# Clustered attention and two MLPs: sums over keys by matrix products, and a new order of the work around a head's value products

## The chip, the cores and the metric

The kernel runs on one core of one Trainium2 chip. The metric is the device time of one launch in microseconds (us). Engines are named as in the profile: PE (TensorE), DVE (VectorE), ACT (ScalarE), POOL (GpSimd), SP (SyncE, which issues DMAs).

## What is computed

Attention over 2 batches x 8 heads, 768 tokens, 64 features, in which a query sees only the keys of its own cluster; then two MLPs over the 1536 tokens. Cut to what matters:

```python
q_assign = argmax(q_n . c_n)            # 16 centroids per head, all normalised
k_assign = argmax(k_n . c_n)
mask = q_assign[:, :, :, None] == k_assign[:, :, None, :]
scores = where(mask, (q . k) / sqrt(D), -1e9)
scores = scores - max(scores, axis=-1)
attn = exp(scores)
attn = attn / (sum(attn, axis=-1) + 1e-9)
x = reshape(attn . v)                   # 1536 x 512
x = (silu(x @ w_in)) @ w_out            # d_ff 2048
out = (sigmoid(x @ w_gate) * (x @ w_val)) @ w_out2   # d_ff 1536
```

## The kernel before

**Tiles.** Heads come in 8 pairs p with j = 0, 1; head h = 2p + j, so there are 16. Tokens are cut into NT = 6 tiles of 128. Every fp32 operand of a product is split into a high part and the rest, so a score is the sum of a product of high tiles `qb`, `kb` (112 rows: 96 of features, 16 of the cluster mask) and one of low tiles `qa`, `ka` (97 rows; the last of `qa` holds the negated maximum of each query). Scores are computed with keys on the partitions, so the sum over keys, the softmax denominator, runs over partitions.

**One head on PE**, in an order written out by hand (`tc.manual_schedule`):

- `leading_maximum(h, i)`, i = 0 to 5 (L456, L466): two products of 384 columns into an `s` tile (two buffers), whose maximum DVE takes into `nm`.
- `shift_row(h, late, w)` (L476): transposes of those maxima into `r`, one for query tiles 0 and 1 (early) and one for tiles 2 to 5 (late); ACT puts them as a row into `qa`.
- `unit(h, u)`, u = 0 to 8 (L490, L497): scores `t`, then exp on ACT into `ring` (`ph` in the rows, two heads deep). Units 0 to 2 need the early row, units 3 to 8 the late one. All `t`, `r`, `pm`, `ps`, `pt` and `n` tiles share three PSUM buffers.
- `values(h)` (L539): 12 fp32 products of 384 columns with `ring`, 24 pieces in the trace.

The value products of head h-1 stand inside head h, after its unit 2 and its last two maxima. They are followed by `denominator_rows(h-2)` (L524), by the late row of head h and by units 3 to 8, among which the first four maxima of head h+1 stand.

**Denominators.** `denominators(h)` (L510 to L513): for each half of the queries DVE adds three key tiles to three (1152 elements a partition), and POOL adds the three results in two steps into `sum`. Six small products with `one_of` (L524) add over the partitions, and ACT casts them to `dn`. `finish(p)` sends both heads' denominators through DRAM, so that DVE can invert them on 96 partitions (`rs`, L569, L570), reads them back broadcast into `rb`, and POOL multiplies (`acc`, L579). The last two heads do without DRAM: `inverse` (L622) adds over the partitions with a tile of ones, and DVE inverts (`rd`).

**The next pair** is prepared meanwhile: cluster products and their turn (`clusters` L153, `turned` L164), `choice` and `one_hot` on DVE (L416 to L429, result `oh`), `mask_rows` (PE L439, ACT L441, four DMAs), `split` (five POOL operations, L404, L68, L407, L408) and DMAs that copy the parts into the tiles (`leading`, `following`, on SP's queue).

The other engines' order is made by a scheduler from the program's order and its own estimates of time; `tc.issue_after(x)` keeps an instruction behind x. Around the last head, weights for the MLPs are loaded and split as well (`ci`, `co`, `wi0a`, `wi0b`, `wo`: ACT, DVE, POOL).

Of the kernel before, what the change touches and what calls it, by code (L numbers as in the profile page):

```python
# [31 lines left out]
def clustered_attention_then_two_mlps(ctx, tc, qT, kT, v, cen, cenT, w1i, w1o, w2g, w2v, w2o, out):  # L32
# [5 lines left out]
    P = 128  # L38
# [72 lines left out]
    with ExitStack() as att:  # L111
# [124 lines left out]
        with tc.issue_after(diagonal.ins):  # L236
            constants(0)
            constants(1)
            one_of = cp.tile([P, GT, D], F32, tag="one_of", name="one_of")
            nc.gpsimd.memset(one_of, 0.0)  # L240
            all_ones = cp.tile([P, D], F32, tag="all_ones", name="all_ones")
            nc.gpsimd.memset(all_ones, 1.0)
            for c in range(GT):
                nc.gpsimd.memset(one_of[:, c, c : c + 1], 1.0)
# [60 lines left out]
        nc.scalar.activation(qh, qq, AF.Copy, scale=scale)  # L305
        cast(nc.scalar, kh, kk)
        nc.vector.tensor_tensor(kl, kk, kh, op=ALU.subtract)
        nc.vector.scalar_tensor_tensor(ql, qq, scale, qh, op0=ALU.mult, op1=ALU.subtract)
# [19 lines left out]

        def first_choice(j, seen):
            sg = seen.rearrange("p (w j c) -> p j w c", j=2, c=C)[:, j]  # L330
            wq, mw = yield from ranked(0, j, sg, 2 * NT)
            for n in range(2):
                nc.vector.tensor_tensor(
                    oh[0][:, :, j, n, 0:C],
                    wq.rearrange("p (t n) c -> p n t c", n=2)[:, n],
                    mw.rearrange("p (t n) -> p n t", n=2)[:, n].unsqueeze(2).to_broadcast([P, NT, C]),
                    op=(ALU.not_equal, ALU.is_equal)[n],
                )
# [17 lines left out]
        def first_masks():  # L356
            with tc.issue_after(maxima[NT - 1].ins):
                for _ in first_choice(1, sums):
                    pass
# [3 lines left out]
            query_rows(1, pt, 0, 0, NT // 2)  # L363
            key_rows(nc.vector, 1, pt, 0, 0, NT)
            query_rows(1, pt, NT // 2, NT // 2, NT // 2)
# [5 lines left out]
        nc.scalar.activation(ex, unit_norm[:, 0:1], AF.Exp)  # L371
        half = NT // 2
# [63 lines left out]
        def mask_rows(p):  # L436
# [5 lines left out]
            for j in range(2):  # L442
                for n, t in enumerate(high[p % 2]):
                    a = 64 * n + 32 * j
                    dma(t[masks, j].bitcast(F32), rows[a : a + C])
# [36 lines left out]
        def unit(h, u):  # L482
# [14 lines left out]
            x = nc.scalar.activation(ring[:, kts[0] : kts[-1] + 1, h % 2, c], t, AF.Exp)  # L497
# [4 lines left out]
        sums_of = {}  # L502

        def denominators(h):

            s = wk.tile([P, S], F32, tag="sum", name=f"sum{h}")
            for g in range(2):
                c = slice(g * G, (g + 1) * G)
                d = wk.tile([P, 3, G], F32, tag="d", name=f"d{h}_{g}", bufs=1)
                nc.vector.tensor_tensor(d, ring[:, 0:3, h % 2, c], ring[:, 3:6, h % 2, c], op=ALU.add)  # L510
                eng = nc.vector if h == NH - 1 else nc.gpsimd
                eng.tensor_tensor(s[:, c], d[:, 0], d[:, 1], op=ALU.add)  # L512
                summed.append(eng.tensor_tensor(s[:, c], s[:, c], d[:, 2], op=ALU.add))  # L513
            sums_of[h] = s

        xf, dn = {}, {}

        def denominator_rows(h, o):

            s = sums_of.pop(h)  # L520
            for c in range(GT):
                for g, r in enumerate((L, U)):
                    at = g * G + c * P
                    nc.tensor.matmul(  # L524
                        o[r], lhsT=one_of[:, c, :], rhs=s[:, at : at + P], start=c == 0, stop=c == GT - 1
                    )
            p, j = divmod(h, 2)
            if p not in dn:
                dn[p] = fin.tile([P, 2, P], F32, tag="dn", name=f"dn{p}", bufs=1)
            r = slice(0, D + GT)  # L530
            cast(nc.scalar, dn[p][r, j], o[r])
# [26 lines left out]
        def finish(p):  # L558

            b, hp = divmod(p, HP)  # L560
            d = dr.tile([2, GT, 2, P], F32, tag="d", name=f"d{p}")
            e = dr.tile([2, GT, 2, P], F32, tag="e", name=f"e{p}")
            n = dn.pop(p)
            dma(d[0], n[0:GT])
            dma(d[1], n[D : D + GT])
            rows = 2 * GT * 16
            rs = fin.tile([P, 16], F32, tag="rs", name=f"rs{p}")
            dma(rs[0:rows], d.rearrange("g c j (a s) -> (g c j a) s", s=16)[0:rows])
            nc.vector.tensor_scalar_add(rs[0:rows], rs[0:rows], 1e-9)  # L569
# [47 lines left out]
        def inverse(h, sums):  # L617

            o = ps_t.tile([P, 512], F32, tag="t", name=f"n{h}")
            for n, s in enumerate(sums):  # L620
                for g, r in enumerate((L, U)):
                    nc.tensor.matmul(  # L622
                        o[r, 0:G],
                        lhsT=all_ones,
                        rhs=s[:, g * G : (g + 1) * G],
                        start=n == 0,
                        stop=n == len(sums) - 1,
                    )
# [24 lines left out]

        shift_row(0, False, P)
        leading_maximum(0, 2)
        clusters(1)
        unit(0, 0)
        leading_maximum(0, 3)
        unit(0, 1)
        leading_maximum(0, 4)  # L660
        unit(0, 2)
        leading_maximum(0, 5)
        turned(1)
        split(1)
# [3 lines left out]
        shift_row(0, True, P)  # L668
        first_masks()
# [4 lines left out]
        def rest_of(h):  # L674

            k = h + 1
            more = k < NH
            for u, i in ((3, 0), (4, 1), (5, None), (6, 2), (7, None), (8, 3)):
                unit(h, u)
                if i is not None and more:  # L680
                    leading_maximum(k, i)
                if u == 6:
                    if h % 2 == 0 and (h + 2) // 2 < NPAIR:
                        mask_rows((h + 2) // 2)
                    if more:
                        shift_row(k, False, P)
                working()

        def prepare(p):
            if p < NPAIR:  # L690
                clusters(p)
# [4 lines left out]
        leading_maximum(1, 0)  # L696
        leading_maximum(1, 1)
        unscaled(0, values(0))
        shift_row(1, False, D)
        choice(1, maxima[NT + 1])  # L700
        one_hot(1, maxima[NT + 1])
        unit(1, 0)
        leading_maximum(1, 2)
        unit(1, 1)
        leading_maximum(1, 3)
        mask_rows(1)
        unit(1, 2)
        leading_maximum(1, 4)
        leading_maximum(1, 5)
        denominators(0)  # L710
        shift_row(1, True, P)
        rest_of(1)
        prepare(2)

        for h in range(2, NH):
            p = (h + 3) // 2
            unit(h, 0)
            denominators(h - 1)
            if h == 2:
                turned(2)  # L720
                for j in range(2):
                    leading(2, j)
                    following(2, j)
            elif p < NPAIR:
                if h % 2:
                    turned(p)
                    leading(p, 0)
                    following(p, 0)
            if h % 2 == 0 and 2 < (h + 2) // 2 < NPAIR:
                leading((h + 2) // 2, 1)  # L730
                following((h + 2) // 2, 1)
            unit(h, 1)
            leading_maximum(h, 4)
            unit(h, 2)
            leading_maximum(h, 5)
            if h == 2:
                choice(2, maxima[-1])
                one_hot(2, maxima[-1])
            elif h % 2 and p < NPAIR:
                choice(p, maxima[-1])  # L740
            elif h % 2 == 0 and (h + 2) // 2 < NPAIR:
                one_hot((h + 2) // 2, maxima[-1])
            o = values(h - 1)
            if h < NH - 1:
                denominator_rows(h - 2, o[:, G:])
                unscaled(h - 1, o)
            else:
                denominator_rows(h - 2, ps_t.tile([P, 512], F32, tag="t", name=f"n{h - 2}")[:, 0:P])
                xo = fin.tile([P, S], F32, tag="xf", name=f"xo{h - 1}")
                cast(nc.scalar, xo[:, 0:G], o[:, 0:G])  # L750
            if h % 2 and h > 1:
                finish((h - 3) // 2)
                if (h - 3) // 2 == HP - 1:
# [537 lines left out]
```

## Time and profile before

| | us |
|---|---|
| three runs | 850.74, 844.76, 850.70 |
| median | 850.7 |
| the profiled execution | 846.96 |
| its span (first to last instruction) | 845.2 |

The span falls into three parts by the starts of the value products: up to those of head 1 (57.8 us), thirteen heads up to those of head 14 (263.3), the way from there into the first MLP (to 318.7, the first product of its second step), and the MLPs. The profile names a tile as written and as read (out<-in), the line of the code, and, for idle time, the instruction that ended it. PEclk is the clock granted to TensorE, 1.00 for 2.4 GHz and 0.50 for 1.2 GHz.

### The profile page before, as it was taken

Reading aid. Unit: us, or ns where it says so; the run is one execution under the profiler, and the core shown is the slowest. Engines: PE = TensorE matmul, PEld = TensorE weight load, DVE = VectorE, ACT = ScalarE, POOL = GpSimd, SP = SyncE. Lnnn points to the kernel's source line nnn. Section 1 sums busy time; section 2 is a strip of 40 time slices with the busy share of each in tenths; the row PEclk is TensorE's granted clock in tenths of the full one; section 3 lists DMA queues with packets and bytes.
Section 4 is the critical chain, followed back from the end, with each engine's and each line's share of the span. In section 5 each row is a group of like instructions: output and inputs, shape, how many; then the busy total and the mean of one; then the engine's idle time right before and its main releaser. Section 6 shows DMA issues by size and latency. Waiting matters only on the chain.

```text
span 845.2 us, 11109 instructions
## 1 busy us (share of the span) xinstructions
PE 774.5 (92%) x4179; PEld 653.5 (77%) x4179; DVE 640.3 (76%) x714; ACT 371.7 (44%) x610; POOL 465.8 (55%) x402
## 2 busy tenths in 40 slices
PE   7788988988797369999999999999999999999997
PEld 3455655655565249989989989999899998989896
DVE  5777777766756697387989778799759697988846
ACT  4435535536354426535435424554643333434220
POOL 3446646649668853434756443544557483948320
PEclk9889999989899579999999999999999999999999
DMA  8745564553511220121322222121111221212004
GB/s 216 184 104 160 131 153 111 141 133 85 144 30 51 69 74 26 51 71 55 115 86 76 74 75 75 50 76 67 58 50 50 75 76 51 100 50 74 1 1 150
DMA packets 32202, 72.26 MB, mean 86 GB/s; under 512 B 6570, under 2 KB 12372, under 8 KB 32148
## 3 DMA queue, kind: packets, MB, share of 16 engines
q1 hardware_dynamic: 31604, 71.52, 28.6%
q8 instruction: 33, 0.54, 0.3%
q14 instruction: 21, 0.17, 0.1%
q10 hardware_dynamic: 544, 0.03, 0.0%
HBM read 48.05 MB, written 3.23 MB: 61 GB/s over the span
## 4 chain that ended last, share of the span: by engine, by line
PE 74%; POOL 7%; DMA 5%; DVE 5%; issue 4%; ACT 2%; SPq 2%; POOLq 0%; DVEq 0%; ACTq 0%
PE z L1107 12%; PE t L490 5%; PE y L1048 4%; PE h_0x L932 3%; PE h_0w L932 3%; PE v L539 3%; PE g_0w L932 2%; PE g_0x L932 2%; PE v_0w L932 2%; PE v_0x L932 2%; PE s L456 2%; PE r L998 2%; PE q L998 2%; PE y_00None L1048 2%; PE y_20None L1048 2%
## 5 line engine op out<-in xcount | busy, mean ns | idle before, releaser
L466 DVE TENSOR_REDUCE nm<-s 128x1 f32<-128x768 f32 x96 | 88.6, 948 | 48.6 <-PE s L456 48.2
L497 ACT ACTIVATE ph<-t 128x512 f32<-128x512 f32 x144 | 82.8, 597 | 35.9 <-PE t L490 35.0
L1107 PE MATMUL z<-wu,ghb 128*128 128x512 f32 (+1 forms) x292 | 89.5, 388 | 0.0
L490 PE MATMUL t<-qa,ka 97*128 97x256 f32 (+1 forms) x192 | 71.6, 383 | 17.3 <-ACT qa L66 13.1
L490 PE MATMUL t<-qb,kb 112*128 112x256 f32 (+1 forms) x192 | 75.0, 401 | 2.3 <-ACT rows L441 2.3
L510 DVE TENSOR_TENSOR d<-ph 128x1152 f32<-128x1152 f32 x30 | 53.6, 1785 | 22.7 <-POOL sum L513 22.7
L539 PE MATMUL v<-ph,vv 128*64 128x384 f32 x384 | 68.9, 500 | 0.0
L512 POOL TENSOR_TENSOR sum<-d 128x384 f32<-128x384 f32 x30 | 30.7, 1024 | 59.6 <-DVE d L510 42.3
L1107 PEld LDWEIGHTS z<-wu,ghb 128*128 128x128 f32 x292 | 54.2, 188 | 11.6 <-ACT ghb L66 0.5
L456 PE MATMUL s<-kb,qb 112*128 112x384 f32 x192 | 53.3, 360 | 8.2 <-DVE nm L466 7.5
L490 PEld LDWEIGHTS t<-qa,ka 97*128 97x128 f32 x192 | 41.4, 216 | 24.4 <-ACT qa L66 22.6
L1107 PE MATMUL z<-wu,glb 128*128 128x512 f32 (+1 forms) x146 | 56.9, 390 | 0.0
L539 PEld LDWEIGHTS v<-ph,vv 128*64 128x64 f32 x384 | 27.3, 139 | 34.2 <-issue 33.7
L490 PEld LDWEIGHTS t<-qb,kb 112*128 112x128 f32 x192 | 41.5, 216 | 12.0 <-ACT rows L441 4.8
L456 PEld LDWEIGHTS s<-kb,qb 112*128 112x128 f32 x192 | 35.6, 204 | 15.3 <-DVE nm L466 10.0
L1028 DVE TENSOR_TENSOR acc<-z,acc 128x1024 f32<-128x1024 f32 (+2 forms) x32 | 36.7, 1153 | 13.9 <-PE z L1107 13.2
L827 POOL TENSOR_TENSOR wo<-co,wo 128x512 fp32r<-128x512 f32 x16 | 23.1, 1449 | 27.0 <-ACT wo L66 27.0
L513 POOL TENSOR_TENSOR sum<-sum,d 128x384 f32<-128x384 f32 x30 | 32.6, 1088 | 0.9
L1048 PE MATMUL y<-gha,wo 128*128 128x384 f32 x128 | 32.8, 334 | 0.0
L1107 PEld LDWEIGHTS z<-wu,glb 128*128 128x128 f32 x146 | 27.4, 188 | 6.9 <-DVE glb L988 1.4
L66 ACT ACTIVATE dn<-v 67x128 f32<-67x128 f32 x13 | 3.6, 273 | 57.4 <-PE v L524 53.7
L808 ACT ACTIVATE co<-ro 128x512 f32<-128x512 f32 x16 | 10.7, 672 | 36.1 <-DMA ro<-in_w1o 33.0
(633 smaller groups left out, 2183.7 us busy)
## 6 DMA issues: line engine op xcount, KB each, us to landing
ri<-in_w1i SPq DMA_DIRECT2D x16, 512.0 KB
ro<-in_w1o SPq DMA_DIRECT2D x16, 512.0 KB, 3.3
rg<-in_w2g SPq DMA_DIRECT2D x12, 512.0 KB, 3.1
rv<-in_w2v SPq DMA_DIRECT2D x12, 512.0 KB, 3.1
ru<-in_w2o SPq DMA_DIRECT2D x12, 512.0 KB, 3.1
qq<-in_qT SPq DMA_DIRECT2D x8, 384.0 KB, 4.8
kk<-in_kT SPq DMA_DIRECT2D x8, 384.0 KB, 4.1
qb<-qh SPq DMA_DIRECT2D x16, 192.0 KB, 2.5
```

Of the source, the lines that this page charges most:

```text
L456: nc.tensor.matmul(s[:, g, 0:HS], lhsT=q[0 : LAST + C, j, i * P : (i + 1) * P], rhs=k[0 : LAST + C, j, g * HS : (g + 1) * HS], start=True, ...
L466: maxima.append(nc.vector.tensor_reduce(n, s[:, :, 0:HS], axis=AX.XY, op=ALU.max, negate=True))
L490: nc.tensor.matmul(t[:, n], lhsT=k[0:rows, j, kt * P : (kt + 1) * P], rhs=q[0:rows, j, c], start=m == 0, stop=m == 1,)
L497: x = nc.scalar.activation(ring[:, kts[0] : kts[-1] + 1, h % 2, c], t, AF.Exp)
L510: nc.vector.tensor_tensor(d, ring[:, 0:3, h % 2, c], ring[:, 3:6, h % 2, c], op=ALU.add)
L513: summed.append(eng.tensor_tensor(s[:, c], s[:, c], d[:, 2], op=ALU.add))
L539: m = nc.tensor.matmul(o[r, 0:G], lhsT=heads[p][:, j, kt, :], rhs=ring[:, kt, h % 2, g * G : (g + 1) * G], start=kt == 0, stop=kt == NT - 1,)
L932: nc.tensor.matmul(o[:, b, 0:HS], lhsT=w[a][s][:, k, :], rhs=right[b, q][t][:, k, :], start=start and k == 0 and n == 0, stop=k == KQ - 1 ...
L998: nc.tensor.matmul(o[:, h, 0:HS], lhsT=w[f"a{m + 1}{r + 1}"][s][:, k, :], rhs=right[b, f"{r + 1}{h + 1}"][t][:, k, :], start=r == 0 and k ...
L1028: added.append(nc.vector.tensor_tensor(z, o, z, op=ALU.add))
L1048: nc.tensor.matmul(o[:, d, 0:width], lhsT=s[:, d, k, :], rhs=t[:, c], start=k == 0 and m == 0, stop=k == 1 and m == 2,)
L1107: nc.tensor.matmul(o[:, a, c], lhsT=s[:, q * P : (q + 1) * P], rhs=r[:, c], start=k == 0 and m == 0, stop=k == 1 and m == 2, skip_group_ch ...
```

## The change

- **Denominators.** DVE adds key tile n+3 to n in three sums of 768 elements into `d` (L513 of the changed kernel). POOL adds nothing any more. PE takes all three in six products of 384 columns with a tile of ones (L522), in a PSUM tile of their own, `n`, from the three shared buffers. They now belong to the head whose values were just taken.
- **Rows of maxima.** All six maxima of head h+1 are computed inside head h's work (`ahead`). The late row of head h is transposed before the value products of head h-1, and the early row of head h+1 right behind them.
- **`split`.** The two high parts are cast on ACT; POOL does the two subtractions alone. The softmax scale moves from `split` into exp.
- **`choice`** for the next pair runs at an even head, `one_hot` and `mask_rows` at the odd head behind it, each one head sooner. `finish` is cut in two: `collect` (to DRAM and back into `rs`) at the even head, the inversion and the rest at the odd one, which held all of it before.
- **The last two heads** have no DVE or POOL sums: `inverse` takes the six key tiles of `ring` directly, twelve products each. That of head 14 stands right behind its values, that of head 15 ahead of its values.
- At the start, maxima come before the first row, and the second head's choice is split in two.

Cut to its core:

```diff
-        def split(p):
+        def split(p, behind=None):
             qq, kk = raws.pop(p)
             qh, ql, kh, kl = parts(p)
-            nc.gpsimd.tensor_scalar(qq, qq, scale, 1.0, op0=ALU.mult, op1=ALU.mult)
-            cast(nc.gpsimd, kh, kk)
-            cast(nc.gpsimd, qh, qq)
-            nc.gpsimd.tensor_tensor(kl, kk, kh, op=ALU.subtract)
-            on_pool["split", p] = nc.gpsimd.tensor_tensor(ql, qq, qh, op=ALU.subtract)
+            cast(nc.scalar, kh, kk)
+            cast(nc.scalar, qh, qq)
...
+                nc.gpsimd.tensor_tensor(kl, kk, kh, op=ALU.subtract)
+                on_pool["split", p] = nc.gpsimd.tensor_tensor(ql, qq, qh, op=ALU.subtract)
...
-        def denominators(h):
...
+        def sums(h):
+
+            d = wk.tile([P, 3, S], F32, tag="d", name=f"d{h}", bufs=1)
+            for n in range(3):
+                summed.append(
+                    nc.vector.tensor_tensor(d[:, n], ring[:, n, h % 2], ring[:, n + 3, h % 2], op=ALU.add)
+                )
+            sums_of[h] = [d[:, n] for n in range(3)]
+
+        def denominators(h, terms):
+
+            o = ps_t.tile([P, 512], F32, tag="t", name=f"n{h}")
+            for n, s in enumerate(terms):
                 for g, r in enumerate((L, U)):
...
+                        o[r, 0:G],
+                        lhsT=all_ones,
+                        rhs=s[:, g * G : (g + 1) * G],
...
+        def inverse(h):
+
+            o = denominators(h, [ring[:, kt, h % 2] for kt in range(NT)])
             rd = fin.tile([P, S], F32, tag="rb", name=f"rd{h}")
...
+        def stretch(h):
+            o = values(h)
+            denominator_rows(h)
+            unscaled(h, o)
...
+        for h in range(2, NH - 1):
...
+            sums(h - 1)
             unit(h, 0)
+            ahead(k, 0)
...
             unit(h, 1)
...
             unit(h, 2)
+            ahead(k, 1)
...
             shift_row(h, True, D)
+            stretch(h - 1)
+            shift_row(k, False, D)
...
+            for u, i in ((3, 2), (4, None), (5, 3), (6, 4), (7, None), (8, 5)):
+                unit(h, u)
+                if i is not None:
+                    ahead(k, i)
...
+        o = values(h - 1)
+        xo = fin.tile([P, S], F32, tag="xf", name=f"xo{h - 1}")
+        cast(nc.scalar, xo[:, 0:G], o[:, 0:G])
+        rd = inverse(h - 1)
         while work:
             working()
         for u in range(3, UNITS):
             unit(h, u)
...
+        scaled_values(h - 1, xo, rd)
+        rd = inverse(h)
+        o = values(h)
         scaled_values(h, o, rd)
```

In the rows of the order below, the number after a name is that of its buffer or tile, which differs between the kernels.

PE around the value products of head 3, before: the products with `one_of` and the late row `r_2` behind them.

```order
L490 MATMUL t_2_939<-qb_141,kb_142 128x256
L490 MATMUL t_2_939<-qa_137,ka_138 128x256
L456 MATMUL s_5_945<-kb_142,qb_141 128x384 x2
L539 MATMUL v_951<-ph,vv_243 64x384 x12
L524 MATMUL v_951<-sum_772,one_of 64x128 x6
L476 MATMUL r_2_974<-ident,nm_868 64x128 x4
L490 MATMUL t_3_982<-qb_141,kb_142 128x512
L490 MATMUL t_3_982<-qa_137,ka_138 128x512
L456 MATMUL s_0_986<-kb_142,qb_141 128x384 x2
```

The same place now:

```order
L494 MATMUL t_2_957<-qb_141,kb_142 128x256
L494 MATMUL t_2_957<-qa_137,ka_138 128x256
L460 MATMUL s_1_963<-kb_142,qb_141 128x384 x2
L480 MATMUL r_2_972<-ident,nm_782 64x128 x4
L546 MATMUL v_978<-ph,vv_238 64x384 x12
L522 MATMUL n_991<-d_921,all_ones 64x384 x6
L480 MATMUL r_0_1001<-ident,nm_934 64x128 x2
L494 MATMUL t_3_1012<-qb_141,kb_142 128x512
L494 MATMUL t_3_1012<-qa_137,ka_138 128x512
L460 MATMUL s_2_1016<-kb_142,qb_141 128x384 x2
L494 MATMUL t_4_1020<-qb_141,kb_142 128x512
```

The late row stands ahead of the values, the early row `r_0` of the next head behind them, and the last maxima product ahead of the row is the second of the next head, `s_1`. Between `s_5` and these rows stand only units 0 to 2 and `s_0`.

DVE before, from the choice at one head to the next head's maxima; `rs` is the inversion:

```order
L466 TENSOR_REDUCE nm_989<-s_5_1104 128x1
L416 TENSOR_REDUCE mk<-sim_1040 128x24
L419 TENSOR_TENSOR eq_1109<-sim_1040,mk 128x384
L422 TENSOR_TENSOR wq_1111<-eq_1109,mk 128x384
L510 TENSOR_TENSOR d_1_1071<-ph 128x1152
L466 TENSOR_REDUCE nm_1162<-s_0_1159 128x1
L569 TENSOR_SCALAR rs_1140<-rs_1140 96x16
L466 TENSOR_REDUCE nm_1162<-s_1_1168 128x1
L570 RECIPROCAL rs_1140<-rs_1140 96x16
L466 TENSOR_REDUCE nm_1162<-s_2_1180 128x1
L466 TENSOR_REDUCE nm_1162<-s_3_1196 128x1
L510 TENSOR_TENSOR d_0_1207<-ph 128x1152
```

DVE now, over the same change of heads:

```order
L470 TENSOR_REDUCE nm_934<-s_4_1048 128x1
L513 TENSOR_TENSOR d_1064<-ph 128x768 x2
L470 TENSOR_REDUCE nm_934<-s_5_1060 128x1
L513 TENSOR_TENSOR d_1064<-ph 128x768
L470 TENSOR_REDUCE nm_1077<-s_0_1074 128x1
L470 TENSOR_REDUCE nm_1077<-s_1_1099 128x1
L427 TENSOR_REDUCE mk<-wq_970 128x24
L583 TENSOR_SCALAR rs_1008<-rs_1008 96x16
L428 TENSOR_TENSOR oh_145<-wq_970,mk 128x24x16
L584 RECIPROCAL rs_1008<-rs_1008 96x16
L470 TENSOR_REDUCE nm_1077<-s_2_1152 128x1
L470 TENSOR_REDUCE nm_1077<-s_3_1175 128x1
```

Three sums now stand together, two of them ahead of the maximum of `s_5` and one behind it. The inversion stands behind the maximum of `s_1` instead of between two maxima that the next early row needs.

ACT where the last head's units 3 to 8 (`t_3` to `t_8`) come, before; `co` is a weight on its way in, `qa<-r_2` the late row:

```order
L497 ACTIVATE ph<-t_2_2497 128x2x256
L66 ACTIVATE wi0a<-ci_0_2677 128x512
L66 ACTIVATE xo_2528<-v_2507 128x384
L66 ACTIVATE wi0b<-ci_1_2685 128x512
L808 ACTIVATE co_0_2731<-ro_0_2729 128x512
L66 ACTIVATE dn_2417<-n_2520 67x128
L66 ACTIVATE qa_139<-r_2_2543 1x512
L497 ACTIVATE ph<-t_3_2549 128x512
L497 ACTIVATE ph<-t_4_2553 128x512
L497 ACTIVATE ph<-t_5_2557 128x512
L808 ACTIVATE co_1_2742<-ro_1_2740 128x512
L497 ACTIVATE ph<-t_6_2561 128x512
```

ACT now:

```order
L501 ACTIVATE ph<-t_2_2435 128x2x256
L66 ACTIVATE qa_139<-r_2_2449 1x512
L66 ACTIVATE wi0a<-ci_0_2611 128x512
L66 ACTIVATE wi0b<-ci_1_2619 128x512
L66 ACTIVATE xo_2468<-v_2455 128x384
L836 ACTIVATE co_0_2665<-ro_0_2663 128x512
L836 ACTIVATE co_1_2676<-ro_1_2674 128x512
L501 ACTIVATE ph<-t_3_2486 128x512
L501 ACTIVATE ph<-t_4_2490 128x512
L501 ACTIVATE ph<-t_5_2494 128x512
L501 ACTIVATE ph<-t_6_2498 128x512
L501 ACTIVATE ph<-t_7_2502 128x512
```

The late row has come ahead of the weights. Both `co` and the cast of head 14's values, `xo`, now stand between it and the exp of unit 3.

## Rows read from the trace of the kernel before

**Rows 1.** Stretches of the span between value starts: length, busy per engine, PEclk, DMA.

```profile
core 0: us, PE busy (x) PEld busy (x) DVE busy (x) ACT busy (x) POOL busy (x), PEclk, DMA share, GB/s
0.00:57.80 57.80, 43.53 (x212) 26.88 (x212) 38.34 (x77) 26.79 (x49) 21.71 (x29) 0.88 0.66 167
...
73.90:88.10 14.20, 12.26 (x79) 8.63 (x78) 10.52 (x13) 7.11 (x15) 5.92 (x5) 1.00 0.54 142
...
104.00:120.80 16.80, 13.80 (x79) 10.15 (x78) 11.76 (x14) 7.27 (x15) 7.02 (x6) 0.90 0.57 148
...
167.00:185.50 18.50, 15.04 (x79) 11.17 (x78) 11.75 (x14) 7.49 (x15) 7.01 (x6) 0.82 0.53 137
...
201.40:220.70 19.30, 14.81 (x79) 10.56 (x78) 14.60 (x15) 7.35 (x15) 12.81 (x10) 0.82 0.39 89
...
263.30:318.70 55.40, 31.43 (x129) 19.48 (x129) 43.60 (x45) 17.54 (x31) 39.33 (x34) 0.69 0.23 74
318.70:845.20 526.50, 522.10 (x2738) 485.48 (x2736) 413.95 (x450) 220.29 (x330) 269.78 (x238) 1.00 0.19 66
```

**Rows 2.** Groups on PE, 57.8 to 263.3: count, busy, mean ns, idle before.

```profile
L456 PE MATMUL s<-kb,qb 112*128 112x384 f32 x157 | 43.0, 356 | 4.6 <-DVE nm L466 4.6
L490 PE MATMUL t<-qb,kb 112*128 112x512 f32 x78 | 34.8, 446 | 2.3 <-ACT rows L441 2.3
L490 PE MATMUL t<-qa,ka 97*128 97x512 f32 x78 | 33.1, 425 | 15.0 <-ACT qa L66 10.7 <-DMA qq<-in_qT 2.1 <-DMA d<-dn 1.1
...
L476 PE MATMUL r<-ident,nm 128*128 128x128 f32 x26 | 6.4, 300 | 5.9 <-DVE nm L466 5.9
```

**Rows 3.** The timeline of DVE at 114.5.

```profile
114.53 0.17 DVE L569 TENSOR_SCALAR rs<-rs 96x16 f32<-96x16 f32 x1 [2.07 <-DMA rs<-d]
```

**Rows 4.** The timeline of PE, 115 to 116, and of 214.

```profile
115.62 0.32 PE L476 MATMUL r<-ident,nm 128*128 128x128 f32 x1 [1.93 <-DVE nm L466]
...
214.05 1.01 PE L456 MATMUL s<-kb,qb 112*128 112x384 f32 x2 [3.43 <-DVE nm L466]
```

**Rows 5.** The stretch around the second of those waits, columns as in rows 1.

```profile
212.60:219.40 6.80, 5.35 (x18) 4.59 (x19) 4.86 (x8) 2.11 (x4) 2.00 (x2) 0.50 0.15 34
```

**Rows 6.** Groups on PE, 263.3 to 318.7, with what ended their idle time.

```profile
L622 PE MATMUL n<-sum,all_ones 128*64 128x384 f32 x4 | 3.1, 874 | 18.1 <-POOL sum L513 18.1
...
L932 PE MATMUL h_0y<-xt,wi0s 128*128 128x384 f32 x6 | 1.4, 369 | 2.4 <-DVE acc L639 2.4
```

**Rows 7.** The chain of waits, 56 to 62.5: start, length, what.

```profile
56.99 0.48 PE t L490 x4
...
57.83 4.02 PE v L539 x24
61.85 0.68 PE v L524 x12
```

**Rows 8.** Durations on DVE: one sum at 6.67, the groups of 57.8 to 263.3, sums at 289.

```profile
6.67 0.96 DVE L307 TENSOR_TENSOR kl<-kk,kh 128x768 fp32r<-128x768 f32 x1 [0.75 <-ACT kh L66]
...
L466 DVE TENSOR_REDUCE nm<-s 128x1 f32<-128x768 f32 x79 | 73.1, 948 | 34.9 <-PE s L456 34.5
...
289.04 6.24 DVE L771 TENSOR_TENSOR ph<-ph 128x768 f32<-128x768 f32 x3
```

**Rows 9.** The timeline of PE at 309.22, a product of the first MLP.

```profile
309.22 1.31 PE L932 MATMUL h_0w<-xt,wi0s 128*128 128x384 f32 x6
```

**Rows 10.** Groups on ACT and POOL, 57.8 to 263.3, and a cast of 768 columns.

```profile
L497 ACT ACTIVATE ph<-t 128x512 f32<-128x512 f32 x118 | 67.4, 597 | 24.0 <-PE t L490 23.2
...
L579 POOL TENSOR_TENSOR acc<-xf,rb 128x768 f32<-128x768 f32 x6 | 10.9, 1814 | 8.0 <-DMA rb<-e 8.0
...
L66 ACT ACTIVATE x<-acc 128x768 fp32r<-128x768 f32 x2 | 1.7, 834 | 1.1 <-DVE acc L639 1.1
```

**Rows 11.** DMA issues: count, KB each, median us to landing.

```profile
kb<-kh SPq DMA_DIRECT2D x16, 192.0 KB, 4.7
...
rb<-e SPq DMA_DIRECT2D x14, 192.0 KB, 3.7
```

More of the change, by code (lines that the diff above doesn't have):

```diff
@@ L357, in first_masks @@
             with tc.issue_after(maxima[NT - 1].ins):
-                for _ in first_choice(1, sums):
+                for _ in second:
                     pass
@@ L371, in clustered_attention_then_two_mlps @@
         nc.scalar.activation(ex, unit_norm[:, 0:1], AF.Exp)
+        second = first_choice(1, sums)
+        next(second)
         half = NT // 2
@@ L441, in mask_rows, with masks_in @@
             nc.scalar.activation(rows, pt[:, 0:S], AF.Identity, bias=rowbias, scale=rowscale)
[L442 to L445, printed above, removed]
+            mask_parts[p] = rows
+            masks_in(p, 0)
+        mask_parts = {}
+        def masks_in(p, j):
+            for n, t in enumerate(high[p % 2]):
+                a = 64 * n + 32 * j
+                dma(t[masks, j].bitcast(F32), mask_parts[p][a : a + C])
         NH = 2 * NPAIR
@@ L672, in clustered_attention_then_two_mlps, with ahead @@
         load(2)
[L674 to L680, printed above, removed]
-                    leading_maximum(k, i)
[L682 to L687, printed above, removed]
+        def ahead(k, *tiles):
+            for i in tiles:
+                if k < NH:
+                    leading_maximum(k, i)
         def prepare(p):
             if p < NPAIR:
-                clusters(p)
                 split(p)
@@ L694, in prepare, with moved_in @@
                     load(p + 1)
-        leading_maximum(1, 0)
-        leading_maximum(1, 1)
-        unscaled(0, values(0))
+        def moved_in(p, j):
+            if p < NPAIR:
+                if j:
+                    masks_in(p, j)
+                leading(p, j)
+                following(p, j)
+        def stretch(h):
+            o = values(h)
+            denominator_rows(h)
+            unscaled(h, o)
+        ahead(1, 0, 1)
+        sums(0)
+        stretch(0)
         shift_row(1, False, D)
-        choice(1, maxima[NT + 1])
@@ L713, in clustered_attention_then_two_mlps @@
         prepare(2)
-        for h in range(2, NH):
-            p = (h + 3) // 2
-            unit(h, 0)
[L718 to L731, printed above, removed]
+        unit(1, 4)
@@ L732, in clustered_attention_then_two_mlps @@
             unit(h, 1)
-            leading_maximum(h, 4)
+            if p < NPAIR and (even or h < 4):
+                turned(p)
             unit(h, 2)
[L735 to L743, printed above, removed]
@@ L762, in clustered_attention_then_two_mlps @@
+        h = NH - 1
+        for u in range(3):
+            unit(h, u)
+        finish((h - 3) // 2, latest[0])
+        shift_row(h, True, D)
+        o = values(h - 1)
+        xo = fin.tile([P, S], F32, tag="xf", name=f"xo{h - 1}")
+        cast(nc.scalar, xo[:, 0:G], o[:, 0:G])
+        rd = inverse(h - 1)
         while work:
```

191 lines of the change are left out of this document (97 added, 94 removed).

## The prediction

> **What bounds the kernel now.** I read the busy times by stretch between value starts first [rows 1]. The MLPs, 526.50 us of the span, have PE busy for 522.10: nothing in attention can shorten them. The thirteen middle heads take 263.3 - 57.8 = 205.5 us. A quiet head of the odd kind, such as the one from 73.90, takes 14.20 us with PE busy for 12.26; three others of that kind take 16.80, 18.50 and 19.30 with PEclk at 0.82 to 0.90. The way into the MLPs is the worst stretch: 55.40 us, PE busy for 31.43, PEclk 0.69. So PE is the engine to count, but with gaps, and each gap is named by a wait.
>
> Second, the waits of PE. In the middle heads the low score products stand idle 15.0 us in all, most of it for the cast of the late row `qa`; the DMA names in that row are waits of the same place, one per head [rows 2]. Transposes and maxima products wait 5.9 and 4.6 us for a maximum, and high score products 2.3 us for the mask rows [rows 2]. On the way into the MLPs 18.1 us go to POOL's sums, in two waits [rows 6].
>
> Third, what a long wait does afterwards. At 114.53 DVE had waited 2.07 us for the denominators' round trip with a maximum queued behind it [rows 3]; PE's transposes then waited 1.93 us [rows 4]. That head, from 104.00, has a mean PEclk of 0.90 [rows 1]. Around the wait of 3.43 us it is 0.50, the 1.2 GHz level, for 6.8 us [rows 4, 5]. The waits for `qa`, about 1.1 us each (15.0 over 13 heads), left PEclk at 1.00 in the quiet head [rows 1, 2].
>
> **Products with ones, middle heads: +17.3 us.** Twelve pieces with `one_of` took 0.68 us, and 24 value pieces of 384 columns 4.02 [rows 7]. The six new products have the value products' columns and number half as many, so 2.01 us. They are on PE, in the path: +1.33 us a head, 13 heads.
>
> **Late row ahead of the values: -15.0 us.** The cast now has 4.02 + 2.01 us of PE work to hide behind, and the early row behind the values is wanted only three quarters of a head later. All of the 15.0 goes [rows 2]. If ACT were held up by more than 6 us there, the wait would come back.
>
> **Round trip and choices moved: -13.7 us.** The inversion now stands behind a round trip issued a head earlier, and DVE no longer waits for POOL. The three long heads exceed 14.2 by 2.6, 4.3 and 5.1, 12.0 together, their slow clock included [rows 1]. The three waits behind them cover some 8 of the 5.9 + 4.6 us for maxima, if the middle one, which has no row here, lay between the two shown [rows 2, 4]; of the 2.7 left I take 1.7 as gone. Mask rows: the wait of 2.3 us may go or stay; I take -1.0.
>
> **Three sums in a row: +11 us, the least certain term.** A maximum takes 0.95 us, a sum of 768 elements 0.96 alone and 6.24 / 3 = 2.08 in the worst row [rows 8]. In the new order `s_1` needs the buffer of `s_5`, and `r_2` its maximum, and that stands on DVE behind two sums. Count from the end of `s_4` on PE. PE wants `s_1` after units 7 and 8, `s_5`, units 0, 1, 2 and `s_0`: five units at 0.48 [rows 7] and two products of 0.36 [rows 2], 3.1 us (a unit of either shape has the same columns). DVE finishes the maximum of `s_4` at about 1.2, two sums at 3.1, the maximum of `s_5` at 4.1. So PE waits about 1.0 us, or 0.45 in the heads where the turn of the next pair's choices stands in between. Exps of 0.60 us feed the sums in time [rows 10]. I take 0.85 a head, which leaves something for sums slowed by POOL, 11 us; the bounds are 0 (DVE gets ahead) and 1.7 a head, +22.
>
> The Trainium skill (SBUF, Who interferes with whom) says that a VectorE instruction with two inputs in SBUF contends with a GpSimd instruction that reads SBUF, and that a VectorE reduction never does. The sums at 0.96 and 2.08 us agree with the first part. By that rule the price depends on what POOL does at the change of heads, which is less than before, since its sums are gone; with two slow sums `s_1` would come 2.2 us later still.
>
> **Casts on ACT: 0.** Two casts of 768 columns, 0.83 us each [rows 10], for each of six pairs, lie inside the value stretch with ACT far from full (7 to 9 us busy of 14 to 16). Bound: a cast that waits for the DMAs that still read its buffer holds up `qa` and the exps; that is a rival below. The scale rides on the exp that is there already: no instruction more.
>
> **Start, to 57.8 us: 0.** The same work, with the rows and choices in another order and two more casts on ACT. Nothing there is priced by a row of its own. The nearest is the late row's wait, 1.1 us at each place: I bound the stretch by -5 and +4.
>
> **The way into the MLPs: -24.7 us.** PE now has: values of head 14, 4.02; 24 pieces with ones, 4.02; six units, 2.9; first MLP product, 1.3; 24 pieces, 4.02; values of head 15, 4.02; five MLP groups at about 1.2 (1.31 with its overlap [rows 9]), 6.0. That is 26.3. POOL's waits of 18.1 go, and with them the slow clock behind them. The wait of 2.4 for `acc` stays [rows 6]. A new one comes: on ACT, exp of unit 3 stands behind two weight casts `co`, the second of which stands behind POOL's weight subtraction, and that behind the `acc` of pair 6. From the start of the values: exp 0.6, inversion 0.5, out to DRAM 2 (an estimate, between 0 and the 3.7 of the way back), back 3.7 [rows 11], `acc` 1.8 [rows 10], a subtraction 1.2 (512 of 768 columns), a cast 0.6: 10.4 us. PE has 4.02 + 4.02 + two units = 9.0 us until it needs a tile that this exp frees. So 1.4, and I take 2. Sum 30.7, against 55.4: -24.7, and 26 to 36 as bounds, the upper with a longer hold-up and a slow stretch like those of [rows 5].
>
> **Sum.** 17.3 - 15.0 - 13.7 - 1.0 + 11 = -1.4 in the middle heads, -24.7 behind, 0 elsewhere: -26.1. The profiled execution took 846.96 us, its span 845.2 and 1.8 around it: 846.96 - 26.1 = 820.9, so 821 us. The runs' median, 850.7, lies 3.7 above that execution; I keep the profiled one as the base.
>
> **Rivals.**
>
> *DVE keeps ahead.* If the maximum of `s_5` comes in time, the 11 us go, and the start may give 4: 806 us. For: DVE loses its waits for POOL. Against: the order, which puts two sums ahead of that maximum. Chance 0.13.
>
> *The new wait grows past the length that brought the slow clock.* By the rule of contention, and by the two waits shown, 1.93 and 3.43 [rows 4]: with sums at 2.08 DVE reaches the maximum of `s_5` at 6.3, and PE waits 3.2. Each such head costs 2.4 more than I take, and 2 to 3 in clock: four heads, about +18, 839 us. For: POOL's subtractions and early operands run late in the heads. Against: it has no sums left. Chance 0.16.
>
> *The way into the MLPs gains only half.* If the weights' chain or the last inversion holds PE by 12 us more than counted (two DMA landings and a slow stretch), 833 us. For: the exps of the last head stand behind a chain that was beside it. Against: 9 us of PE work cover it. Chance 0.14.
>
> *The casts block ACT: slower.* A cast of a new pair's high part must wait until the DMAs that read the old one have landed, 4.7 us for the longest [rows 11], and they are queued with a dozen others on SP. On ACT the late row and the exps stand behind it. Six pairs; from 26.1 / 6 = 4.4 us a pair on, the kernel is no faster; with 6 us and a slow stretch of 3.4 [rows 5] it would be 821 + 56 = 877 us. For: six casts that nothing but the scheduler's estimate places. Against: they stand two heads behind those DMAs. Chance 0.04.
>
> **How the numbers follow.** The forecast has the rest, 0.53, and its own range is 812 to 830. The range, 802 to 841, takes in the first three rivals and leaves out the last and the tails of the others. About 1% is what a measurement of this kernel can tell from no change, here 842 to 859. Forecast and the first three rivals lie below it but for a part of the slow-clock case: faster 0.92, same 0.04, slower 0.04.
>
> **What would show it.** Right: no wait of the low products for `qa`, products with ones near 2.0 us, a wait of `s` for a maximum of 0.5 to 1.2 us in nearly every head, PEclk at 1.00 in all middle heads, and about 31 us from the values of head 14 to the second step of the MLP. Wrong: PEclk at 0.50 in several heads behind that wait; sums with a mean above 1.5 us; an ACT cast of `kh` or `qh` with a long idle time for a DMA ahead of it; PE idle for exps of the last head by 10 us.

## The result, and the profile after

The changed kernel takes 817.89 us (median of 4 runs, 812.84 to 821.43), the kernel before beside it 847.73: ratio 0.9646, 95% interval 0.9573 to 0.9718. A second set of four runs gave 816.41 (810.63 to 819.40) and 0.9638 [0.9593, 0.9683]. The forecast was 821, range 802 to 841. Its profile has a span of 815.4 us against 845.2.

The stretches of the changed kernel, cut at the same events as [rows 1]: start to the values of head 1, thirteen heads, the way into the MLP's second step, the rest (columns as in [rows 1]):

```profile
0.00:58.50 58.50, 46.63 (x232) 29.41 (x232) 35.79 (x83) 30.30 (x54) 12.20 (x15) 0.88 0.76 194
58.50:259.50 201.00, 187.87 (x1104) 120.61 (x1103) 135.49 (x160) 115.06 (x211) 65.07 (x38) 0.97 0.44 111
259.50:289.00 29.50, 27.49 (x146) 15.54 (x146) 19.27 (x25) 14.82 (x26) 17.64 (x17) 0.94 0.28 85
289.00:815.40 526.40, 522.17 (x2737) 485.15 (x2735) 421.98 (x458) 222.86 (x335) 281.74 (x247) 1.00 0.20 69
```

Against 57.8, 205.5, 55.4 and 526.5 us: +0.7, -4.5, -25.9 and -0.1. So the gain is nearly all in the way into the MLPs, where PE is now busy for 27.49 of 29.50 us. In the thirteen heads PE is busy for 187.87 us of 201.00, more than before, and waits less.

What is left of PE's waits in the thirteen heads, and then in the way into the MLPs (total, times, longest), to be held against [rows 2] and [rows 6]:

```profile
PE s L460 <- DVE nm L470: 13.1, 12, 2.9
...
PE t L494 <- ACT ph L501: 1.5, 1, 1.5
PE h_0v L960 <- DVE h_0u L983: 0.5, 1, 0.5
```

The waits for `qa`, for the mask rows, of the early row's transposes and for POOL's sums are gone; one new wait is there, twelve times: `s_1` stands still until DVE has taken the maximum of `s_5`. The way into the MLPs on PE's timeline:

```profile
259.46 4.09 PE L546 MATMUL v<-ph,vv 128*64 128x384 f32 x24
263.38 4.04 PE L522 MATMUL n<-ph,all_ones 128*64 128x384 f32 x24
...
271.60 0.50 PE L494 MATMUL t<-qb,kb 112*128 112x512 f32 x1 [1.50 <-ACT ph L501]
...
273.26 5.71 PE L522 MATMUL n<-ph,all_ones 128*64 128x384 f32 x24
278.81 4.04 PE L546 MATMUL v<-ph,vv 128*64 128x384 f32 x24
...
287.74 1.31 PE L960 MATMUL h_0v<-xt,wi0b 128*128 128x384 f32 x6 [0.51 <-DVE h_0u L983]
288.89 4.32 PE L1026 MATMUL p<-x,wi0a 128*128 128x384 f32 x24
```

The two waits that made up the 18.1 us of [rows 6] in the kernel before have no successor but the 1.50 us for an exp:

```profile
286.01 1.54 PE L622 MATMUL n<-sum,all_ones 128*64 128x384 f32 x2 [5.03 <-POOL sum L513]
...
300.58 0.90 PE L622 MATMUL n<-sum,all_ones 128*64 128x384 f32 x1 [13.02 <-POOL sum L513]
```

### The profile page after: what moved, and what is told of

It reads as the page before. It is cut to its first block, busy times and chain, and to the rows that moved or that the text cites. A ratio compares the mean times of both kernels' runs of the same rounds, so it can differ in the third digit from the quotient of the medians.

```text
span 815.4 us, 11135 instructions
## 1 busy us (share of the span) xinstructions
PE 784.2 (96%) x4211; PEld 650.7 (80%) x4211; DVE 612.5 (75%) x723; ACT 383.1 (47%) x623; POOL 376.6 (46%) x317
## 4 chain that ended last, share of the span: by engine, by line
PE 85%; DVE 9%; DMA 3%; SPq 1%; ACT 1%; issue 1%; DVEq 0%; ACTq 0%
PE z L1135 12%; PE v L546 7%; PE y L1076 4%; DVE nm L470 4%; PE n L522 4%; DVE d L513 4%; PE t L494 4%; PE h_0w L960 3%; PE h_0x L960 3%; PE s L460 3%; PE g_0w L960 3%; PE g_0x L960 3%; PE v_0w L960 3%; PE v_0x L960 3%; PE r L1026 2%; PE q L1026 2%
## 5 line engine op out<-in xcount | busy, mean ns | idle before, releaser
L494 PE MATMUL t<-qb,kb 112*128 112x256 f32 (+1 forms) x192 | 67.9, 365 | 1.5 <-ACT ph L501 1.5
L494 PE MATMUL t<-qa,ka 97*128 97x256 f32 (+1 forms) x192 | 64.5, 348 | 3.8 <-ACT qa L66 3.7
L591 POOL TENSOR_TENSOR acc<-xf,rb 128x768 f32<-128x768 f32 x7 | 12.9, 1839 | 103.9 <-DMA rb<-e 87.7
L513 DVE TENSOR_TENSOR d<-ph 128x768 f32<-128x768 f32 x42 | 49.5, 1202 | 3.7 <-ACT ph L501 3.7
L494 PEld LDWEIGHTS t<-qb,kb 112*128 112x128 f32 x192 | 37.6, 196 | 8.4 <-ACT ph L501 3.1
L494 PEld LDWEIGHTS t<-qa,ka 97*128 97x128 f32 x192 | 37.7, 196 | 5.7 <-ACT qa L66 4.3
L406 POOL TENSOR_TENSOR kl<-kk,kh 128x768 fp32r<-128x768 f32 x7 | 12.8, 1832 | 58.3 <-ACT kh L66 55.7
L66 ACT ACTIVATE xf<-v 64x384 f32<-64x384 f32 x28 | 13.5, 484 | 37.7 <-PE v L546 37.5
L522 PE MATMUL n<-d,all_ones 128*64 128x384 f32 x168 | 29.5, 486 | 0.0
```

Source lines behind the costliest of these rows:

```text
L494: nc.tensor.matmul(t[:, n], lhsT=k[0:rows, j, kt * P : (kt + 1) * P], rhs=q[0:rows, j, c], start=m == 0, stop=m == 1,)
L513: nc.vector.tensor_tensor(d[:, n], ring[:, n, h % 2], ring[:, n + 3, h % 2], op=ALU.add)
L522: nc.tensor.matmul(o[r, 0:G], lhsT=all_ones, rhs=s[:, g * G : (g + 1) * G], start=n == 0, stop=n == len(terms) - 1,)
```

## The experiments

Each kernel ran beside the kernel before, on the same chip, in three groups; the kernel before had a median of 846.2 to 846.3 us in all three. Ratios are to it, with their 95% intervals; differences between two kernels are of medians. A quiet head is one of those, early among the thirteen, in which POOL has little to do and PEclk is 1.00.

**The changed kernel again.** No edit.

> The changed kernel as it is, so that the other runs of this chip have it beside them. 818 us, between 812 and 822, with 13 us of PE waiting for maxima in the middle heads.

816.41 us, 0.9638 [0.9593, 0.9683]; waits for maxima in the thirteen heads 13.4 us. This is the measure for the runs below.

**Where the new wait comes from: the order on DVE.** All three sums behind the maximum of `s_5`:

```diff
             for n in range(3):
-                summed.append(
+                with tc.issue_after(maxima[-1].ins):
+                    summed.append(
```

> All three VectorE sums of a head are kept behind the maximum of s_5. Theory (the order on VectorE makes the new wait): PE's waits for maxima in the middle heads fall from 13.1 us to under 3, and the slow stretches at 181, 212 and 242 us, 13.6 us at half clock, go: -10 and -7, about 801 us. Rival (VectorE is simply full at the change of heads): the sums now push the maxima of s_0 and s_1 and the products with ones, the wait moves there, 814 to 822 us.

795.22 us (794.21 to 796.53), 0.9397 [0.9374, 0.9420]: 21 us less than the changed kernel, and a version that beats both. Its stretches, from the values of head 1 and of head 14, and PE's waits in the thirteen heads:

```profile
56.70:239.30 182.60, 179.49 (x1104) 117.54 (x1103) 135.58 (x162) 115.17 (x210) 65.08 (x38) 1.00 0.50 125
239.30:267.70 28.40, 26.39 (x149) 15.61 (x149) 21.46 (x27) 14.68 (x26) 18.25 (x17) 1.00 0.27 88
```

```profile
PE pt L438 <- DVE oh L428: 1.4, 1, 1.4
PE s L460 <- DVE nm L470: 1.0, 1, 1.0
PE r L480 <- DVE nm L470: 0.5, 1, 0.5
```

The 201.0 us of the thirteen heads (196.7 in the repeat) became 182.6, and PEclk is 1.00 in both stretches. Waits went from 13.1 to 2.9 us; of the rest up to 6.8 us is clock, since the changed kernel had 13.6 us at half clock there. DVE is as busy as it was (135.58 and 135.49), so it was never full: two sums stood in front of the one maximum for which PE waited. The theory holds, and gave more than it forecast (795 us for 801).

**What makes four of the waits long: POOL beside the sums.** In the changed kernel the waits are 0.24 or 0.62 us in eight heads, and 1.81, 2.24, 2.88 and 2.39 in four. DVE at a short one and at a long one, and POOL at the long one:

```profile
114.86 1.82 DVE L513 TENSOR_TENSOR d<-ph 128x768 f32<-128x768 f32 x2
...
144.15 3.39 DVE L513 TENSOR_TENSOR d<-ph 128x768 f32<-128x768 f32 x2
147.46 0.95 DVE L470 TENSOR_REDUCE nm<-s 128x1 f32<-128x768 f32 x1
```

```profile
144.00 1.84 POOL L591 TENSOR_TENSOR acc<-xf,rb 128x768 f32<-128x768 f32 x1 [17.00 <-DMA rb<-e]
```

A first try kept POOL's product behind the sums by the scheduler alone:

```diff
+            def scaled():
+                with tc.issue_after(summed[-1].ins):
+                    on_pool["scaled", p] = nc.gpsimd.tensor_tensor(acc[:, hp, :, b, :], *x, op=ALU.mult)
...
             sums(h - 1)
+            while waiting:
+                waiting.pop(0)()
```

> GpSimd's product acc and the early operands that follow it are kept behind the VectorE sums of the head, the sums stay where they are. Theory (GpSimd beside the sums makes four of the waits long): the two sums ahead of the maximum take 1.9 us in all odd heads instead of 3.4 to 4.1, the waits of 1.8 to 2.9 us fall to 0.2 to 0.7, and the slow stretches behind them go: -8 and -7, about 803 us. Rival (the sums are slow by themselves there, or the product then meets the next head's sums): 814 to 822 us.

816.28 us, 0.9649 [0.9603, 0.9695], waits 12.6 us. It tells nothing, for the overlap stayed: `issue_after` did not make POOL wait for DVE. The product started at 143.24, DVE's sums at 143.72, and two sums took 3.06 us. The second try moves the data instead: the inversion one head later, so that `rb` lands later.

```diff
-                finish((h - 3) // 2, last)
...
             sums(h - 1)
+            if even and h >= 4:
+                finish((h - 4) // 2, summed[-1])
```

> The changed kernel with the inversion of a pair one head later, behind the sums of the even head, so that GpSimd's product acc comes well behind the change of heads; the sums stay where they are. Theory (GpSimd's work beside the two sums makes the long waits): at the change of heads around 148 us, where only the product is there, the two sums take 1.9 us instead of 3.2 and PE waits 0.2 instead of 1.6; where early operands follow, around 179 and 210, the waits may stay. 810 to 816 us. Rival (not GpSimd): the wait at 148 stays above 1.2 us.

819.66 us, 0.9680 [0.9631, 0.9729], not the 810 to 816 of the theory. DVE at the change of heads that had the long wait, and at the next one, POOL there, and PE at both:

```profile
144.47 1.82 DVE L513 TENSOR_TENSOR d<-ph 128x768 f32<-128x768 f32 x2
...
158.44 3.45 DVE L513 TENSOR_TENSOR d<-ph 128x768 f32<-128x768 f32 x2
```

```profile
158.54 2.54 POOL L591 TENSOR_TENSOR acc<-xf,rb 128x768 f32<-128x768 f32 x1 [2.58 <-DMA rb<-e]
```

```profile
147.21 0.62 PE L460 MATMUL s<-kb,qb 112*128 112x384 f32 x2 [0.24 <-DVE nm L470]
...
162.82 0.62 PE L460 MATMUL s<-kb,qb 112*128 112x384 f32 x2 [2.25 <-DVE nm L470]
```

With POOL gone from the first place the two sums take 1.82 us and PE waits 0.24 us. The product now meets the next change of heads: the sums there take 3.45, and that wait, 0.62 before, is 2.25 us. The other three long waits left their places too, where PE now waits 0.24, 0.61 and 0.62 us; the next change of heads behind two of them has 2.81 and 2.43. And a product that had ended as the sums began (at 114.91) now makes a wait of 2.26, at 130.43, where 0.61 was. Taking the overlap away and putting it elsewhere moved the waits with it, so the cause is shown; the kernel as a whole got no better, since the overlap only moved.

**The late row's place.** Back behind the values and the products with ones:

```diff
-            shift_row(h, True, D)
             stretch(h - 1)
+            shift_row(h, True, D)
             shift_row(k, False, D)
```

> The late row goes back behind the value products and the products with ones. Theory (its place ahead of the values is worth what the trace of before showed): PE waits about 1.1 us for the cast qa in each of 13 heads, +14 us, about 832 us. Rival (the row waits for the same maximum as s_1, so the place takes as much as it gives): the wait for the maximum shrinks by as much, 816 to 822 us.

824.48 us, 0.9750 [0.9705, 0.9796]: 8 us slower than the changed kernel, between theory and rival. In a quiet head it costs 0.5 us (14.47 for 13.97), not 1.1. ACT shows why: behind the changed kernel's long products with ones the two casts `xf` are over when the row comes, and only `dn` stands ahead of it:

```profile
107.58 0.98 ACT L66 ACTIVATE xf<-v 64x384 f32<-64x384 f32 x2 [4.73 <-PE v L546]
109.50 0.49 ACT L66 ACTIVATE dn<-n 65x384 f32<-65x384 f32 x1 [0.94 <-ACT xf L66]
110.02 0.85 ACT L66 ACTIVATE qa<-r 1x512 fp32r<-1x512 f32 x2
```

In the kernel before, whose products took 0.68 us, `xf` stood between:

```profile
92.95 0.27 ACT L66 ACTIVATE dn<-v 67x128 f32<-67x128 f32 x1 [4.49 <-PE v L524]
93.24 0.98 ACT L66 ACTIVATE xf<-v 64x384 f32<-64x384 f32 x2
94.24 0.59 ACT L66 ACTIVATE qa<-r 1x512 fp32r<-1x512 f32 x1
```

The same move alone, in the kernel before:

```diff
+            shift_row(h, True, D)
             o = values(h - 1)
...
-            shift_row(h, True, D)
```

> The kernel before with one part of the change: the late row transposed ahead of the value products, all else as it was. Theory (the place alone gives the 15 us): the waits of the low products for qa go, 832 us. Rival (the row then waits for the maximum of s_5, which stands right ahead of it on PE): the waits for qa go, but PE waits about 1.1 us a head for that maximum, 843 to 850 us.

842.62 us, 0.9960 [0.9931, 0.9990]. PE's longer waits in the middle heads:

```profile
PE r L476 <- DVE nm L466: 18.8, 21, 4.6
PE s L456 <- DVE nm L466: 2.4, 2, 2.0
```

The 15.0 us for `qa` are gone, but the late row now waits 18.8 us for the last maxima, those of `s_4` and `s_5`; with the 5.9 us of the early row, which are gone, that is 12.9 more. This is the rival, if a little below its 843 us. Alone the place is worth under 4 us, with the maxima taken a head ahead 8.

**The price of the products with ones.** Only one of the three terms goes through them, so the denominators are incomplete:

```diff
-            o = denominators(h, sums_of.pop(h))
+            o = denominators(h, sums_of.pop(h)[:1])
```

> Of the three sums of heads 0 to 13 only the first goes through the products with ones (two products of 384 columns instead of six); the denominators are incomplete, the VectorE sums all stay. Theory (these products lie on PE's path at their full length): -1.34 us in 14 heads, -19, about 799 us. Rival (VectorE's chain sets the length of a head): PE's waits for maxima grow by as much, 814 to 820 us.

800.26 us, 0.9461 [0.9428, 0.9494]: 16 us less, of 19. In quiet heads it is 12.7 us for 13.97 and 14.3 for 15.30. The products lie on PE's path at nearly full length, and the rival is out: PE's waits for maxima in the thirteen heads did not grow (12.8 us for 13.4). What is missing of the 19 was not traced; the start alone is 1.8 us longer in this profile than in the repeat (59.25 for 57.46).

**The ending alone,** in the kernel before:

```diff
+                rd_last = inverse(h - 1, [ring[:, kt, (h - 1) % 2] for kt in range(NT)])
...
-        o = values(h, range(3))
-        rd = inverse(h, [partial_sums[:, n] for n in range(3)])
-        values(h, range(3, NT), o)
+        rd = inverse(h, [ring[:, kt, h % 2] for kt in range(NT)])
+        o = values(h)
```

> The kernel before with one part of the change: the denominators of the last two heads by twelve products with ones on the six key tiles each, no VectorE or GpSimd sums for them. Theory (most of the gain is there): the stretch from the values of head 14 to the MLP falls from 55.4 to about 31 us, 823 us. Rival (the old order around it keeps POOL or ACT in the way): the stretch stays above 43, 836 us or more.

828.73 us, 0.9795 [0.9759, 0.9832]: 17.5 us less than the kernel before, and in its profile the stretch is

```profile
262.70:297.10 34.40, 30.69 (x164) 19.39 (x164) 24.09 (x32) 14.90 (x26) 20.30 (x19) 0.90 0.23 74
```

21.0 us shorter than 55.4, and 5 longer than in the changed kernel, 3.66 of them a wait of a product of the first MLP for ACT at 291. The theory holds, but for those 5 us: most of the gain there is this one part of the change.

**Casts on ACT or on POOL.** First those of pairs 1 and 2, then all:

```diff
-            cast(nc.scalar, kh, kk)
-            cast(nc.scalar, qh, qq)
+            cast(nc.gpsimd if p < 3 else nc.scalar, kh, kk)
+            cast(nc.gpsimd if p < 3 else nc.scalar, qh, qq)
```

> The casts of the pairs 1 and 2 go back to GpSimd, those of later pairs stay on ACT. Theory (at the start the casts hold ACT's queue while they wait for DMAs): the PE waits of 3.77 us at 22.4 and 3.31 us at 39.6 go with the slow stretches there, the values of head 1 start 5 to 10 us sooner, 808 to 813 us. Rival (other waits there end as late): 815 to 820 us.

> The casts of all pairs go back to GpSimd. Theory: as with the first two pairs at the start, and in the middle heads GpSimd has some 3 us more to do in every second head, away from the sums: the mean of a sum stays within 0.1 us of 1.20, 808 to 813 us. Rival (GpSimd's added work meets the sums): the mean of a sum rises above 1.35 us, the waits for maxima by 5 us or more, and the gain of the start is gone, 816 to 822 us.

817.15 us, 0.9652 [0.9601, 0.9702], and 814.34, 0.9624 [0.9589, 0.9658]: neither can be told from 816.41. In the changed kernel ACT does stand still at the start:

```profile
20.32 0.84 ACT L66 ACTIVATE kh<-kk 128x768 fp32r<-128x768 f32 x1 [3.66 <-DMA qa<-ql]
...
35.96 0.84 ACT L66 ACTIVATE qh<-qq 128x768 fp32r<-128x768 f32 x1 [6.14 <-DMA qq<-in_qT]
```

and PE waits 3.77 and 3.31 us behind it. With the first casts on POOL the values of head 1 start at 54.4 instead of 57.5. That is no clear gain: with the casts on ACT they start anywhere from 55.7 (the inversion later) to 59.3 (one product), and nothing shows in the time. So neither theory's 808 to 813 us came. With all casts on POOL the mean of a sum is 1.26 us, as with none (1.25), so the rival of added contention falls as well. To see the start without the heads' waits, the sums behind the maximum and the first casts on POOL together:

> sums_behind and casts_pool_first together: the sums behind the maximum of s_5, the casts of pairs 1 and 2 on GpSimd. Theory (the start's waits for ACT's casts are real, and were hidden in the earlier run by slow stretches that differ from run to run): without those, the values of head 1 start some 4 us sooner, 791 us against the 795 of sums_behind. Rival (the start gains nothing by it): 795 us.

793.83 us (792.95 to 796.69), 0.9384 [0.9334, 0.9434], not to be told from 795.22. PE's longer waits from 25 to 60 us, of this kernel and of the one with the sums behind alone:

```profile
PE s L460 <- DMA kb<-rows: 5.5, 1, 5.5
PE pm L153 <- DMA qq<-in_qT: 1.4, 1, 1.4
PE t L494 <- ACT qa L66: 1.1, 2, 0.6
```

```profile
PE t L494 <- ACT qa L66: 5.0, 2, 4.5
```

The wait for ACT's cast turned into one for the mask rows' DMA: the values of head 0 begin 2.7 us sooner (25.7 for 28.4), those of head 1 no sooner (57.6 for 56.7). What would shorten those transfers was not tried.

**One product less for one sum more.** VectorE adds two of the three sums, in the kernel with both edits (sums behind the maximum, first casts on POOL):

```diff
+                summed.append(nc.vector.tensor_tensor(d[:, 0], d[:, 0], d[:, 1], op=ALU.add))
+            sums_of[h] = [d[:, n] for n in (2, 0)]
...
-            last = maxima[-1]
+            last = summed[-1]
```

> As both, and VectorE adds two of a head's three sums once more, so that the products with ones take two terms: four products of 384 columns instead of six. Theory (these products lie on PE's path, VectorE has room once the sums stand behind the maximum): -0.67 us in 14 heads, -9 against both, about 783 us; the sum more, 1 us a head, is hidden. Rival (VectorE's chain then sets the head): the products or the next maxima wait for the fourth sum, 790 us or more.

800.74 us, 0.9456 [0.9408, 0.9505]: 7 us slower than without, the rival. A quiet head of one kind gains what the theory says (14.15 us for 14.81), the one behind it nothing (13.6 for 13.5, with 0.9 us of waiting for ACT's `dn`), and where POOL runs beside it the fourth sum comes late. PE's longer waits, and DVE before the longest of them:

```profile
PE n L525 <- DVE d L517: 7.3, 3, 3.1
PE pt L438 <- DVE oh L428: 3.1, 1, 3.1
PE t L494 <- ACT dn L66: 1.1, 2, 0.9
```

```profile
206.73 2.41 DVE L517 TENSOR_TENSOR d<-d 128x768 f32<-128x768 f32 x1
```

## Why the prediction was right, and where not

**The way into the MLPs,** forecast -24.7, came to -25.9, and the ending alone shows 21.0 of it. The mechanism is the one forecast: POOL's sums are gone from PE's path. Two of its smaller steps were off. The exps of the last head were held up by 1.50 us (2 forecast), but not by POOL's chain behind `acc`: ACT's two weight casts waited for their own transfers.

```profile
269.03 0.68 ACT L836 ACTIVATE co<-ro 128x512 f32<-128x512 f32 x1 [4.88 <-DMA ro<-in_w1o]
270.39 0.67 ACT L836 ACTIVATE co<-ro 128x512 f32<-128x512 f32 x1 [0.68 <-DMA ro<-in_w1o]
270.97 3.02 ACT L501 ACTIVATE ph<-t 128x512 f32<-128x512 f32 x6
```

The round trip of the inversion of pair 6 did hold them, by another way: on SP's queue. The chain of waits (start, length, what; L589 issues `rb`, L830 `ro`):

```profile
258.83 2.94 DMA e<-rs
...
261.79 0.58 SPq L589
...
263.11 0.54 SPq L830
...
263.75 6.57 DMA ro<-in_w1o
```

So the exps came 11.5 us after the start of the values (259.46 to 270.97) where 10.4 were worked out, from other parts: that the sizes agree is luck. And the wait of 2.4 us for `acc`, which was to stay, has no row left, since the last inversion now runs beside the last values; the 0.51 us that PE still waits is for a tile of the MLP. A stretch at half clock (0.50 from 273.2 to 276.6) took back 1.7: the second products with ones took 5.71 for 4.04.

**The thirteen heads,** forecast -1.4, came to -4.5, by terms of which several were off:

- Products with ones, +17.3: right. Twelve pieces take 2.04 us from start to start (93.24 to 95.28 in head 3), and leaving four of six away gave 16 of 19 us.
- The late row, -15.0: right in sum, wrong in cause. Its place is worth 0.5 us a head beside the long products, which already cover the casts ahead of it, and 15.0 less 12.9 without the new order of maxima.
- The new wait, +11: 13.1 measured, by two errors that nearly cancel. Its make is as worked out, two sums ahead of the maximum of `s_5`, but it is not one size. Most heads have 0.24 or 0.62 us where 0.45 or 1.0 was worked out: sums and maxima follow each other on DVE at 0.87 us (114.86 to 116.60 for two), not at 0.95. Four heads have 1.8 to 2.9, where POOL's product or early operands run. That is the rival with a chance of 0.16, in part: three of the four are followed by stretches at 0.50, 3.4, 3.4 and 6.8 us long, which the likeliest case left out and which cost up to half their length, 6.8 us.
- Round trip, choices, mask rows, -14.7: the waits behind them, 5.9 + 4.6 + 2.3 us, are gone from their places; the mask rows' 2.3 went whole, where I took 1.0. With them went 17.0 us at half clock, up to 8.5 in time, so this term was worth up to 21.3.

So the new wait cost up to 19.9 us with its clock where 11 stood in the sum, and the old ones gave up to 21.3 where 14.7 stood. That the heads came near the forecast is in part luck.

In busy time PE has 10.4 us more (187.87 for 177.43), where the products and the shorter slow stretches (13.6 for 17.0 us) would give 15.6. Fewer waits can take most of the difference. A piece ahead of a wait counts with 0.48 us, where pieces in a row start 0.24 apart, and the piece behind it is 0.1 longer (0.50 for 0.40): up to 0.34 a wait. PE had 26 waits in the thirteen heads and has 12, which gives up to 4.8 of the 5.2 us. This is an estimate; it was not tried.

**Start:** +0.7 for 0, but not for want of a change: PE is busy for 3.1 us more (46.63 for 43.53) and idle for 2.4 less. Its trace has the rival of blocked casts in small: ACT's casts do wait for DMAs, 3.66 and 6.14 us, and hold PE. In the middle heads they never do so in PE's path. The rival that ended slower is ruled out there by the waits: none of PE's 13.1 us is for ACT.

**The signs.** Of those named for right, the products with ones and the way into the MLPs (29.5 us for about 31) came, and no wait for `qa` is left; a wait of 0.5 to 1.2 us came in five heads only, and PEclk was not 1.00 in all. Of those for wrong, two came in part: 0.50 behind the new wait, three times, and ACT casts that waited for DMAs, though not in PE's path in the middle heads.

The Trainium skill (SBUF — State Buffer, Who interferes with whom) says that a VectorE instruction with two inputs in SBUF and a GpSimd instruction that reads it shut each other out, while a reduction is not touched. The runs agree: two sums took 1.82 us without POOL and 3.45 beside its product, while a maximum in the changed kernel took 0.94 us though POOL was at work from before it to behind it:

```profile
175.46 5.02 POOL L78 TENSOR_TENSOR x<-acc,x 128x768 fp32r<-128x768 f32 x2
...
178.73 0.94 DVE L470 TENSOR_REDUCE nm<-s 128x1 f32<-128x768 f32 x1
```

In the repeated run POOL's product ended at 144.70 (142.85 + 1.85), and two sums that had started at 143.17 ended at 146.38, 1.7 us behind it: nearly their own length.

## What to carry to other kernels

When an engine takes its work in a fixed order, put first what the bounding engine waits for: the same sums behind one maximum instead of ahead of it were worth 21 us, with the engine no less busy. Price a moved step together with what stands ahead of it on every engine: the row moved alone exchanged 15.0 us of one wait for 12.9 us of others. And a hint to the scheduler made no wait between two engines here; to keep two engines apart in time, move the data that starts one of them, and look at what it meets instead.

## What the runs showed of the hardware

A wait of PE of the same length was followed by half clock in one execution and not in another. In the changed kernel the wait of 2.24 us at 179.73 is followed by the first row below; in its repeat that of 2.23 us at 178.55 by the second:

```profile
181.00:184.40 3.40, 3.40 (x14) 1.25 (x12) 3.37 (x5) 1.99 (x3) 1.31 (x1) 0.50 0.52 118
```

```profile
179.50:182.90 3.40, 3.40 (x24) 1.57 (x24) 3.37 (x5) 2.16 (x3) 1.09 (x1) 1.00 0.62 137
```

The profile of the changed kernel has 13.6 us at half clock in the thirteen heads, that of its repeat 3.4, and the profiled executions took 817.65 and 810.63 us. The spread of a kernel's runs does not simply go with its waits: it is 8.6 us for the changed kernel (812.84 to 821.43) and 2.3 for the one with the sums behind, whose waits there are at most 1.4 us, but also 2.1 for the one with one product, whose waits reach 2.8. What makes the spread stays open.
